# Spare products, copies, mixture pieces and weight sums moved in the first units of a fused RWKV-7 and mixture kernel

## The chip, the cores and the metric

The kernel runs on one core of a Trainium2 chip. The metric is the time of one execution on the device in microseconds, the median of several runs. The profile is of one execution and has its own time.

## The reference

Two blocks follow each other. The first is a recurrence over 768 time steps, for 4 batches of 8 heads, head size 40; each head keeps a 40 x 40 state S:

```
y[t]  = r[t] . S
Sa    = S . a[t]
S     = S * w[t] (by column) - outer(Sa, b[t]) + outer(v[t], k[t])
```

The outputs are laid side by side by head into x, 3072 rows (tokens) of 320. The second block is a mixture of 4 experts, all of them applied to every row, weighted by probabilities that are normalised by row:

```
p   = domain_probs / (sum(domain_probs) + 1e-9)
out = sum over e of p[:, e] * (relu(x @ w1[e]) @ w2[e])       w1[e]: 320 x 1024, w2[e]: 1024 x 320
```

Everything is float32.

## The kernel before

**Units.** The time axis is cut into 12 chunks of 64 steps. A unit is one chunk of two batches (all 16 heads of them), so there are 24 units; the units with an even and an odd number carry the two halves of the batches. Inside a chunk the recurrence is written as matrix products, with a triangular system of 64 x 64 per head to solve. A unit goes through these stages, each a generator that is advanced a step at a time:

- `within` (L412): what needs no state. The decays G are accumulated by a scan, turned to token order on TensorE (`pg`), inverted on VectorE (`gp`, a reciprocal), and multiplied into B and K, giving `n_tok` and `k_tok`. These are turned back (`turned`, tiles `pNT` and `pKT`, through `turn`, L359), and V and R as well (`turn_rv`, `pVT` and `pRT`, in units 0 to 2 on TensorE, later by VectorE's transposes). Products give the score matrices `pfe`, `pe` and `pc`, which are masked into F, ET and VC, and `pev`, copied to EV.
- `substitute` (L627), here called the solve: the 32 x 32 diagonal blocks of F are copied (`copy_blocks`, L619, for units 0 and 1), turned into M, and solved by forward substitution in Z. Units 0 and 1 are solved on VectorE, the later ones on GpSimd (POOL) while earlier units go on. The blocks below the diagonal go to the tile `below`.
- `merge` (L704): Z is turned into Qc and QTc; two products, `pY` and `pQ`, give the off-diagonal block of the inverse. QT collects it: the diagonal quarters from QTc (`diagonal`, on ScalarE for units 1 to 5, else on POOL), the others from `pQ`.
- `step` (L750): what needs the state. `prn` (not in the first chunk), `psat` and `pst`, `pxr`, then `pdy`, from which come the output Y and the next state. For the first four units Y is turned into xT by products with a matrix of ones (`pick`, built by `set_pick` with 14 selects on POOL, in the tile `sums` of the last expert); `pxT` is its result.
- the mixture: for units 0 and 1 by unit (`mixture_of_unit`, L930), then by chunk (`mixture_of_chunk`). Its work is cut into pieces in the list `todo`: an `ups(e)` makes the hidden layer of one expert (`ph`, then a relu on ScalarE to `hs`), a `down(e)` multiplies with w2 (`po`) and adds into `osb` with the gate on VectorE. From the second chunk on, the second product is a seven-product scheme, which needs sums of blocks of w2: `add_weights` (L984), 20 VectorE operations, of which some overwrite w2.

**Order.** For units 0 to 5 (`EARLY`) the order of TensorE is the order of the program; most operations on the other engines are pinned in the same way (`keep_in_program_order`), and the rest is placed by a scheduler. The first two units are written out by hand (L1150 to L1255), the others in a loop, in which `gap` (L1272) runs some of the sums (`sums_at`) and then one or two mixture pieces, to fill TensorE while the other engines work. In the solve of unit 1 the function `during_second` (L1217) puts pieces and parts of unit 2 between the 16 substitution steps. `keep_warm` (L1132) and `keep_warm_quadrants` issue products of the identity whose result nobody reads, called spare products here.

**Transfers.** Nearly all loads are issued in order by one queue (SP): the inputs of a unit some units ahead, the first weights in pieces (`load_piece`, 640 KB each), and w2 by expert (`load_w2`, 1280 KB each; that of the last expert only after the solve of unit 1, which uses its tile as room for M and Z).

All matrix products are issued from one helper line, L76, the turns from L79, so they are told apart by their tiles.

Of the kernel before, what the change touches and what calls it, by code (L numbers as in the profile page):

```python
# [15 lines left out]
def kernel(  # L16
# [38 lines left out]
    nc = tc.nc  # L55
# [303 lines left out]
    def turn(name, src, pinned=False):  # L359

        p = big(name)
        for j in range(NJ):
            ins = transpose(out=p[:, j * P:(j + 1) * P], in_=src(j), identity=ident[:])
            if pinned and j == 0:
                tc.keep_in_program_order(ins)
        return p
# [45 lines left out]
    def within(q):  # L412
# [69 lines left out]
        def turned(name, x):  # L482
            t = sb.tile([P, NJ, P], FP32, name=name, tag="turned", bufs=3)
            p = turn("p" + name, tok(x), q.u == 1)[:]
            for js in (slice(0, NJ // 2), slice(NJ // 2, NJ)) if q.u == 0 else (slice(0, NJ),):
                ins = nc.scalar.copy(out=t[:, js], in_=p.rearrange("p (j t) -> p j t", t=P)[:, js])
                if q.u < 2:
                    tc.keep_in_program_order(ins)
            return t
# [44 lines left out]
        if q.u > 0:  # L534
            ins = nc.scalar.copy(out=q.VC[:, :, 0:D], in_=token_V())
            if q.u == 1:
                tc.keep_in_program_order(ins)
# [30 lines left out]
        if q.u == 0:  # L568
            copy_F()
            yield  # L570
            KT = turned("KT", q.K)
        if q.apart or q.u == 0:
            p = banks("pe")
# [11 lines left out]
        if q.u < 2:  # L585
            selected(ET[:], of_slot, pe)
            copy_below(q)
# [4 lines left out]
        if q.u == 0:  # L592
            tc.keep_in_program_order(nc.scalar.copy(out=q.VC[:, :, 0:D], in_=token_V()))
        q.EV = EVs()
# [10 lines left out]
        if q.u == 0:  # L605
            VT = turn_rv()
            yield
# [11 lines left out]
    def copy_blocks(q):  # L619
        blocks = sb.tile([P, H, Q], FP32, name="blocks")  # L620
        for n, (i, s) in enumerate((i, s) for i in range(P // Q) for s in range(2)):
            move = nc.scalar.copy if n >= 5 else nc.vector.tensor_copy
            to, src = of_slot(blocks[quarter(i)], s), q.pf[s][quarter(i), :, quarter(i % 2)]
            tc.keep_in_program_order(move(out=to, in_=src))
        return blocks

    def substitute(q, eng, during=None):  # L627
# [14 lines left out]
        if q.u < 2:  # L642
            unit_columns(nc.gpsimd)
            yield
            blocks = copy_blocks(q)
            yield
        else:
            blocks = sb.tile([P, H, Q], FP32, name="blocks")
            for i in range(P // Q):
                move = nc.scalar.copy if i >= 2 else nc.vector.tensor_copy  # L650
                tc.keep_in_program_order(move(out=blocks[quarter(i)], in_=q.F[quarter(i), :, quarter(i % 2)]))  # L651
            q.below = belows()
            for i in (1, 3):
                move = nc.scalar.copy if q.u <= EARLY else nc.gpsimd.tensor_copy
                tc.keep_in_program_order(move(out=q.below[quarter(i)], in_=q.F[quarter(i), :, 0:Q]))  # L655
# [48 lines left out]
    def merge(q):  # L704
# [16 lines left out]
        on_scalar = 0 < q.u <= EARLY  # L721
# [4 lines left out]
        def two_heads(name, lhsT, rhs, to):  # L726
            p = big(name)
            for n in range(NJ):
                for r in range(2):
                    matmul(  # L730
                        out=p[half(r), n * 2 * Q:(n + 1) * 2 * Q], lhsT=lhsT[half(r), 2 * n:2 * n + 2, :],
                        rhs=rhs[half(r), 2 * n:2 * n + 2, :], start=True, stop=True,
                    )
            for r in range(2):
                for y in range(2):
                    src = p[quarter(2 * r + y), 0:H * Q].rearrange("p (n two t) -> p n two t", two=2, t=Q)[:, :, y, :]
                    ins = nc.scalar.copy(out=of_slot(to[quarter(2 * r)], y), in_=src)  # L737
                    if q.u == 0:
                        tc.keep_in_program_order(ins)
# [190 lines left out]
    def mixture_of_unit(q):  # L930
# [3 lines left out]
        def ups(e):  # L934
# [6 lines left out]
            def piece():  # L941
                lead()
                hs[e] = [up_main(at + 2 * e, q.xT, P, ph[0])]
                hs[e].append(up_main(at + 2 * e + 1, q.xT, P, up_last(at + 2 * e + 1, q.xT, P)))
# [6 lines left out]
            piece.lead = lead  # L951
            return piece
# [14 lines left out]
        todo.append(ups(0))  # L967
        for e in range(E):
            todo.append(lambda e=e: down(e))
            if e + 1 < E:  # L970
                todo.append(ups(e + 1))
# [186 lines left out]
    keep_warm(8)  # L1158
# [10 lines left out]
    run(ws[0], 1)  # L1169
    set_pick()  # L1170
    run(solve)
    keep_warm(16)
    run(ws[0], 3)
    keep_warm(5)
    run(ws[0])
    run(norm, 1)
    keep_warm(4)
    run(ws[1], 1)
    keep_warm(20)
# [9 lines left out]
    keep_warm_quadrants(1)  # L1189
# [3 lines left out]
    run(ws[1], 1)  # L1193
# [13 lines left out]
    run(ws[1], 1)  # L1207
    run(solve, 1)
    run(s, 1)
# [7 lines left out]
    def during_second(j):  # L1217
        if j == 0:
            run(s)
        if j == 4:  # L1220
# [3 lines left out]
            mix(1)  # L1224
        if j == 8:
# [24 lines left out]
    run(m)  # L1250
    run(s, 2)
    run(ws[2])
# [6 lines left out]
    sums_at = {4 * 2 + n: 1 for n in range(1, 11)}  # L1259
    sums_at.update({4 * 4 + 3: 2, 4 * 5 + 0: 3, 4 * 5 + 1: 2, 4 * 5 + 2: 3})  # L1260
# [122 lines left out]
```

## Time and profile before

| | |
|---|---|
| median of 3 runs | 1106.63 us (1103.67 to 1109.6) |
| profiled execution | 1105.66 us |
| its span, first to last instruction | 1103.8 us |
| TensorE busy (PE) | 1077.6 us, 98% |
| VectorE (DVE), ScalarE (ACT), GpSimd (POOL) busy | 753.9, 367.1, 496.7 us |
| mean granted TensorE clock | 0.992 |
| DMA, mean | 111 GB/s, 122.18 MB |

Times in the views count from the first instruction. PE is the matrix products, PEld the weight loads, SPq the issue of a transfer on the SP queue. A row such as `L681 DVE TENSOR_TENSOR w<-w` names the line, the engine, the operation, and the tiles written and read. A float32 product appears as two rows, so 20 spare products are 40 rows. A bracket behind a row gives the idle time of the engine before it and what ended it; "issue" there means that the profile shows nothing that was waited for. The granted clock is a share of full speed.

### The profile page before, as it was taken

What the parts mean: (1) busy time and instruction counts of PE and PEld (TensorE: products, weight loads), DVE (VectorE), ACT (ScalarE), POOL (GpSimd) and SP (SyncE); (2) the same over time, 40 slices, a digit from 0 to 9 for tenths busy, and PEclk for the clock granted to TensorE, in tenths of its full rate; (3) what the DMA queues carried; (4) which work ended last, traced back from release to release, by engine and by line L of the source; (5) the groups of instructions that cost most, each with busy time, mean ns of one, the idle gap of its engine ahead of it and who ended that gap; (6) DMA issues with size and microseconds to landing.
All of it is one profiled execution on the core that took longest, in us unless ns stands there. A gap on an engine that the chain in (4) does not pass through costs nothing.

```text
span 1103.8 us, 38664 instructions
## 1 busy us (share of the span) xinstructions
PE 1077.6 (98%) x16158; PEld 963.5 (87%) x16158; DVE 753.9 (68%) x1546; ACT 367.1 (33%) x998; POOL 496.7 (45%) x1257
## 2 busy tenths in 40 slices
PE   7899899999999999999999999999999999999998
PEld 6777778888999899999989989999998989988887
DVE  7665578887776767767768677767777677543343
ACT  3343555243233243233232342332332342321110
POOL 6215465672653643744634635536537447330000
PEclk8999999999999999999999999999999999999999
DMA  7876625434454364353454443453543532222320
GB/s 145 210 191 172 141 53 151 96 92 122 99 124 112 102 142 106 93 146 93 102 124 114 102 120 89 125 126 78 132 102 84 147 85 67 97 71 77 101 81 12
DMA packets 268868, 122.18 MB, mean 111 GB/s; under 512 B 213736, under 2 KB 242072, under 8 KB 268696
## 3 DMA queue, kind: packets, MB, share of 16 engines
q1 hardware_dynamic: 264872, 119.02, 43.1%
q8 instruction: 127, 2.08, 0.8%
q10 hardware_dynamic: 3824, 0.71, 0.4%
q14 instruction: 45, 0.37, 0.1%
HBM read 111.79 MB, written 3.93 MB: 105 GB/s over the span
## 4 chain that ended last, share of the span: by engine, by line
PE 86%; DVE 5%; ACT 3%; POOL 2%; SPq 2%; issue 2%; DMA 1%; DVEq 0%; ACTq 0%; POOLq 0%
PE ph L76 36%; PE p L76 28%; PE po L76 3%; PE pdy L76 3%; PE psat L76 2%; PE pxr L76 2%; PE prn L76 1%; PE pc L76 1%; PE pQ L76 1%; PE pfe L76 1%; PE warm L76 1%; POOL Z L697 1%; PE pev L76 1%; PE pe L76 1%; PE pY L76 1%
## 5 line engine op out<-in xcount | busy, mean ns | idle before, releaser
L76 PE MATMUL ph<-xT,w1p 128*128 128x256 f32 (+3 forms) x3040 | 443.5, 376 | 3.1 <-issue 1.5
L76 PEld LDWEIGHTS ph<-xT,w1p 64*64 64x64 f32 (+1 forms) x3040 | 336.8, 161 | 70.9 <-issue 25.5
L697 POOL TENSOR_TENSOR Z<-Z 128x31 f32<-128x31 f32 (+7 forms) x704 | 259.0, 368 | 55.2
L1028 DVE TENSOR_TENSOR a<-hs 128x512 f32<-128x512 f32 x220 | 151.9, 708 | 108.3 <-ACT hs L907 108.3
L681 POOL TENSOR_TENSOR Z<-M,Z 128x62 f32<-128x62 f32 (+7 forms) x352 | 142.6, 405 | 150.2 <-DVE M L672 124.3
L907 ACT ACTIVATE hs<-ph 128x512 f32<-128x512 f32 (+1 forms) x208 | 115.1, 564 | 223.4 <-PE ph L76 222.4
L76 PE MATMUL p<-sums,a 128*128 128x160 f32 x1056 | 164.9, 299 | 0.0
L76 PEld LDWEIGHTS p<-sums,a 128*128 128x128 f32 x1056 | 152.8, 190 | 2.2
L920 DVE SCALAR_TENSOR_TENSOR osb<-p,gate,osb 128x320 f32<-128x320 f32 (+1 forms) x243 | 108.3, 482 | 57.7 <-PE p L76 53.4
L76 PE MATMUL p<-w,a 128*128 128x160 f32 x704 | 106.0, 301 | 0.4 <-ACT hs L907 0.4
L76 PE MATMUL p<-w,hs 128*128 128x160 f32 x704 | 102.9, 299 | 0.0
L76 PEld LDWEIGHTS p<-w,hs 128*128 128x128 f32 x704 | 100.2, 190 | 2.2
L76 PEld LDWEIGHTS p<-w,a 128*128 128x128 f32 x704 | 98.3, 190 | 3.3 <-ACT hs L907 3.3
L655 POOL COPY below<-F 32x256 f32<-32x256 f32 x36 | 17.3, 480 | 178.9 <-ACT F L563 177.8
L657 DVE STREAM_TRANSPOSE M<-blocks 128x1024 f32<-128x1024 f32 x23 | 45.4, 1975 | 39.5 <-ACT blocks L651 38.9
L819 ACT COPY RS<-pxr 64x256 f32<-64x256 f32 x88 | 32.3, 367 | 103.6 <-DVE SX L410 42.0
L719 POOL COPY QT<-QTc 32x256 f32<-32x256 f32 x76 | 43.0, 566 | 36.1 <-DVE QTc L711 26.0
L600 ACT COPY EV<-pev 64x160 f32<-64x160 f32 x96 | 23.4, 287 | 87.5 <-PE pev L76 87.0
L478 DVE RECIPROCAL gp<-gp 128x320 f32<-128x320 f32 x23 | 49.5, 2152 | 0.7
L709 DVE STREAM_TRANSPOSE Qc<-Z 128x256 f32<-128x256 f32 x23 | 14.5, 629 | 43.7 <-POOL Z L697 43.6
L737 ACT COPY QT<-pQ 32x128 f32<-32x128 f32 x96 | 24.7, 257 | 58.3 <-PE pQ L76 56.5
L76 PE MATMUL pdy<-VC,k_tok 64*64 64x104 f32 (+1 forms) x768 | 38.2, 260 | 1.4 <-issue 1.4
(169 smaller groups left out, 1382.2 us busy)
## 6 DMA issues: line engine op xcount, KB each, us to landing
w1p<-in_moe_w_dram SPq DMA_DIRECT2D x95, 512.0 KB
w1p<-in_moe_w_dram SPq DMA_DIRECT2D x190, 64.0 KB
w<-in_moe_w_dram SPq DMA_DIRECT2D x4, 1280.0 KB
sums<-in_moe_w_dram SPq DMA_DIRECT2D x9, 512.0 KB
natW<-in_w_dram SPq DMA_DIRECT2D x48, 80.0 KB
natB<-in_b_dram SPq DMA_DIRECT2D x48, 80.0 KB
natK<-in_k_dram SPq DMA_DIRECT2D x48, 80.0 KB
out_dram<-osb SPq DMA_DIRECT2D x46, 80.0 KB
```

The lines of the kernel that those rows point to most:

```text
L76: return stated(nc.tensor.matmul(**k))
L478: pin(nc.vector.reciprocal(out=gp[:], in_=gp[:]))
L600: ins = nc.scalar.copy(out=of_slot(q.EV[half(p)], i ^ p)[:, :, 0:D], in_=pev[i][half(p)])
L657: ins = nc.vector.transpose(out=M[:], in_=cols)
L681: ins = eng.tensor_tensor(out=Z[:, 1:3, 0:n, j + 1:Q], in0=M[:, j:j + 2, None, j + 1:Q].to_broadcast([P, 2, n, m]), in1=Z[:, here, 0:n, j: ...
L697: eng.tensor_tensor(out=z[:, 0], in0=z[:, 0], in1=z[:, x], op=ALU.add)
L719: tc.keep_in_program_order(move(out=q.QT[quarter(i), :, quarter(i % 2)], in_=QTc[quarter(i)]))
L737: ins = nc.scalar.copy(out=of_slot(to[quarter(2 * r)], y), in_=src)
L819: nc.scalar.copy(out=RS[half(s), x ^ s::2], in_=prs[x][half(s)].rearrange("p (j i) t -> p j i t", i=2),)
L907: nc.scalar.activation(out=h[:, i * HF // 2:(i + 1) * HF // 2, 0:n], in_=ph[i][:], func=ACTF.Relu,)
L920: nc.vector.scalar_tensor_tensor(out=to, in0=p, scalar=sc, in1=to, op0=ALU.mult, op1=ALU.add)
L1028: nc.vector.tensor_tensor(out=t[:], in0=x, in1=y, op=op)
```

## The change

The change has seven parts, nearly all in the first two units.

1. Spare products: four and two go into the turn `pNT` of unit 0 (behind its second and fourth transpose), six behind the turn `pKT`; the counts elsewhere change from 14, 8, 16, 5, 4, 20 to 14, 9, 7, 3, 24, and one pair of `keep_warm_quadrants` goes.
2. In unit 0, V and R are turned ahead of `pev`, `copy_below` comes behind EV's copies, and `set_pick` behind the masks of unit 0.
3. `copy_blocks` gives the four copies of one bank to VectorE and the four of the other to ScalarE, where VectorE had five and ScalarE three.
4. `pQ` of unit 0 goes to two banks, and two of the four QT copies to VectorE.
5. Order in the merges: the step of unit 1 that holds `pNT` and `pKT` comes behind `pdy` of unit 0, `pfe` behind `pxT`, and the copies for ET ahead of the relus. In the merge of unit 1 one `ups` is cut in two (`first`, `second`) and run there, so that the `down` behind it moves one gap ahead.
6. For units 2 to 5, the copies to `below` and the diagonal copies to QT go from ScalarE to POOL.
7. The 20 sums lie in 15 gaps (1, 2 or 1 each) where they lay in 14 (1 each, then 2, 3, 2, 3).

The diff, without unchanged context:

```diff
-    def turn(name, src, pinned=False):
+    def turn(name, src, pinned=False, spare={}):
...
+            if spare.get(j):
+                keep_warm(spare[j])
...
-            p = turn("p" + name, tok(x), q.u == 1)[:]
+            p = turn("p" + name, tok(x), q.u == 1, {1: 4, 3: 2} if q.u == 0 and name == "NT" else {})[:]
...
-            if q.u == 1:
+            if q.u < PADDED:
                 tc.keep_in_program_order(ins)
...
             KT = turned("KT", q.K)
+            keep_warm(6)
...
             selected(ET[:], of_slot, pe)
-            copy_below(q)
+            if q.u == 1:
+                copy_below(q)
...
             tc.keep_in_program_order(nc.scalar.copy(out=q.VC[:, :, 0:D], in_=token_V()))
+            VT = turn_rv()
+            yield
         q.EV = EVs()
...
         if q.u == 0:
-            VT = turn_rv()
-            yield
+            copy_below(q)
...
-        for n, (i, s) in enumerate((i, s) for i in range(P // Q) for s in range(2)):
-            move = nc.scalar.copy if n >= 5 else nc.vector.tensor_copy
-            to, src = of_slot(blocks[quarter(i)], s), q.pf[s][quarter(i), :, quarter(i % 2)]
-            tc.keep_in_program_order(move(out=to, in_=src))
+        for i in range(P // Q):
+            for s, move in enumerate((nc.vector.tensor_copy, nc.scalar.copy)):
+                to, src = of_slot(blocks[quarter(i)], s), q.pf[s][quarter(i), :, quarter(i % 2)]
+                tc.keep_in_program_order(move(out=to, in_=src))
...
-                move = nc.scalar.copy if q.u <= EARLY else nc.gpsimd.tensor_copy
-                tc.keep_in_program_order(move(out=q.below[quarter(i)], in_=q.F[quarter(i), :, 0:Q]))
+                tc.keep_in_program_order(nc.gpsimd.tensor_copy(out=q.below[quarter(i)], in_=q.F[quarter(i), :, 0:Q]))
...
-        on_scalar = 0 < q.u <= EARLY
+        on_scalar = q.u == 1
...
-            p = big(name)
+            apart = q.u == 0 and name == "pQ"
+            ps_ = banks(name) if apart else [big(name)] * 2
...
-                    ins = nc.scalar.copy(out=of_slot(to[quarter(2 * r)], y), in_=src)
+                    move = nc.vector.tensor_copy if apart and r else nc.scalar.copy
+                    ins = move(out=of_slot(to[quarter(2 * r)], y), in_=src)
...
-            def piece():
+            def first():
                 lead()
                 hs[e] = [up_main(at + 2 * e, q.xT, P, ph[0])]
+
+            def second():
                 hs[e].append(up_main(at + 2 * e + 1, q.xT, P, up_last(at + 2 * e + 1, q.xT, P)))
...
-            return piece
+            return [first, second] if q.u == 0 and e == E - 1 else [piece]
...
-    keep_warm(8)
+    keep_warm(9)
     run(solve, 1)
...
+    run(solve)
+    run(ws[0], 2)
+    keep_warm(7)
+    run(ws[0], 1)
+    keep_warm(3)
+    run(ws[0])
     set_pick()
-    run(solve)
-    keep_warm(16)
-    run(ws[0], 3)
-    keep_warm(5)
-    run(ws[0])
     run(norm, 1)
-    keep_warm(4)
     run(ws[1], 1)
-    keep_warm(20)
+    keep_warm(24)
...
-    keep_warm_quadrants(1)
     run(ws[1], 1)
     run(m)
     keep_warm_quadrants(1)
-    run(ws[1], 1)
     load_w2(1)
...
     run(s, 1)
     run(ws[1], 1)
+    run(s, 1)
+    run(ws[1], 1)
     run(solve, 1)
-    run(s, 1)
+    run(ws[1], 1)
     mixture_of_unit(units[0])
...
             go(load_raw(begin(3), "W"))
-            mix(1)
-        if j == 8:
+        if j in (6, 8):
             mix(1)
...
     run(m)
+    mix(1)
     run(s, 2)
+    mix(1)
     run(ws[2])
...
-    sums_at = {4 * 2 + n: 1 for n in range(1, 11)}
-    sums_at.update({4 * 4 + 3: 2, 4 * 5 + 0: 3, 4 * 5 + 1: 2, 4 * 5 + 2: 3})
+    sums_at = {4 * 2 + n: 1 if n < 6 or n > 10 else 2 for n in range(1, 16)}
```

More of the change, by code (lines that the diff above doesn't have):

```diff
@@ L730, in two_heads @@
                     matmul(
-                        out=p[half(r), n * 2 * Q:(n + 1) * 2 * Q], lhsT=lhsT[half(r), 2 * n:2 * n + 2, :],
+                        out=ps_[r][half(r), n * 2 * Q:(n + 1) * 2 * Q], lhsT=lhsT[half(r), 2 * n:2 * n + 2, :],
                         rhs=rhs[half(r), 2 * n:2 * n + 2, :], start=True, stop=True,
@@ L735, in two_heads @@
                 for y in range(2):
-                    src = p[quarter(2 * r + y), 0:H * Q].rearrange("p (n two t) -> p n two t", two=2, t=Q)[:, :, y, :]
-                    ins = nc.scalar.copy(out=of_slot(to[quarter(2 * r)], y), in_=src)
+                    src = ps_[r][quarter(2 * r + y), 0:H * Q].rearrange("p (n two t) -> p n two t", two=2, t=Q)[:, :, y, :]
+                    move = nc.vector.tensor_copy if apart and r else nc.scalar.copy
+                    ins = move(out=of_slot(to[quarter(2 * r)], y), in_=src)
                     if q.u == 0:
@@ L949, in piece @@
                     load_w2(e + 2)
-            piece.lead = lead
-            return piece
+            def piece():
+                first()
+                second()
+            piece.lead = first.lead = lead
+            return [first, second] if q.u == 0 and e == E - 1 else [piece]
         def down(e):
@@ L965, in down @@
                 stores.append(lambda: store(q, q.osb))
-        todo.append(ups(0))
+        todo.extend(ups(0))
         for e in range(E):
@@ L970, in mixture_of_unit @@
             if e + 1 < E:
[L971 removed]
+                todo.extend(ups(e + 1))
     def of_w2(e, q, x):
```

## The prediction

> **What bounds the kernel now.** I read the page first (busy time, then the slices), then the busy time by stretches, then the first 115 us engine by engine in order of time. The page:
>
> ```profile
> PE 1077.6 (98%) x16158; PEld 963.5 (87%) x16158; DVE 753.9 (68%) x1546; ACT 367.1 (33%) x998; POOL 496.7 (45%) x1257
> PE   7899899999999999999999999999999999999998
> ```
>
> TensorE is the bound, but not everywhere. Busy time by stretches (second column the length, then PE, its weight loads, DVE, ACT, POOL, granted clock, DMA share, GB/s):
>
> ```profile
> 0.00:28.00 28.00, 20.60 (x234) 18.81 (x234) 22.04 (x56) 8.56 (x25) 17.90 (x56) 0.88 0.75 147
> 28.00:56.00 28.00, 25.12 (x423) 22.54 (x416) 18.57 (x47) 10.37 (x32) 5.70 (x9) 0.94 0.83 210
> 56.00:83.00 27.00, 24.44 (x327) 19.38 (x325) 17.77 (x40) 11.20 (x33) 5.31 (x7) 0.94 0.71 190
> 83.00:110.00 27.00, 25.32 (x359) 20.98 (x354) 15.95 (x38) 9.18 (x29) 16.28 (x48) 0.94 0.62 175
> 330.00:1104.00 774.00, 769.17 (x11114) 695.52 (x11112) 511.98 (x1043) 236.47 (x624) 330.40 (x843) 1.00 0.40 101
> ```
>
> From 330 us on TensorE idles 4.8 us of 774 at full clock; its work there is the same in both kernels. So the change is worth what it takes out of the first 140 us (idle TensorE, half-clock stretches, spare products on the path), and each microsecond won there should reach the end.
>
> TensorE in order of time (start, length, count; the bracket is idle time before and who ended it):
>
> ```profile
> 12.91 0.69 PE L76 MATMUL pfe<-NT,AT 64*64 64x64 f32 x32 [0.55 <-ACT NT L486]
> 15.85 1.13 PE L76 MATMUL pe<-AT,KT 64*64 64x64 f32 x32 [1.66 <-ACT KT L486]
> 16.92 6.36 PE L76 MATMUL warm<-ident 128*128 128x128 f32 x32
> ...
> 28.00 0.65 PE L79 MATMUL pp<-ident,sums 24*128 24x24 f32 x4
> ...
> 31.75 4.98 PE L76 MATMUL warm<-ident 128*128 128x128 f32 x40
> 36.66 0.68 PE L76 MATMUL pY<-QTc,below 64*64 64x64 f32 x16
> ...
> 51.02 2.65 PE L76 MATMUL ph<-xT,w1p 64*64 64x128 f32 x32 [1.42 <-ACT xT L861]
> ...
> 57.99 0.30 PE L76 MATMUL pev<-VC,ET 64*64 64x40 f32 x2 [1.74 <-DVE gl L450]
> 58.71 0.61 PE L76 MATMUL pev<-VC,ET 64*64 64x40 f32 x27 [0.41 <-POOL ET L500]
> ...
> 59.80 6.24 PE L76 MATMUL po<-w,hs 128*128 128x320 f32 x16
> ```
>
> And VectorE:
>
> ```profile
> 31.45 0.45 DVE L711 STREAM_TRANSPOSE QTc<-Qc 128x256 f32<-128x256 f32 x1
> ...
> 66.08 0.55 DVE L918 TENSOR_SCALAR osb<-po,gate 128x320 f32<-128x320 f32 x1 [6.14 <-PE po L76]
> ```
>
> Three things to see. First, QTc is ready at 31.90, yet pY, which needs it, starts at 36.66: it queues behind 20 spare products (40 rows, 4.98 us). Second, TensorE waits 1.74 + 0.41 us before pev of unit 1, because ACT makes ET's copies only after four hs activations; the next po runs at half clock (6.24 us; the same form at full clock takes 4.47). Third, VectorE's solve of unit 1 sits 6.14 us behind that po.
>
> **Part by part.**
>
> *Blocks split by bank.* Five DVE copies (0.258 us each from 13.65) then three on ACT to 15.40 become four and four on different banks: done at 13.65 + 4 x 0.258 = 14.7. The solve of unit 0 (15.44 to 31.90, 16.46 us) ends at about 31.25: -0.65. Unit 1 gets the same.
>
> *Spare products in the first N turn.* Four warm products (0.244 us each at full clock) fit between n_tok's halves (11.0 to 11.95 against 11.92 now), two before pfe end at 12.9 (pfe starts at 12.91), six before pe end at about 15.6 (pe starts at 15.85). On the path: 0 to +0.1. They are for the clock: here it is 0.5 from 15.3 to 22.2, 29.0 to 32.4, 59.7 to 63.2 and 94.0 to 97.4, each stretch one or two times 3.4 us and each after 3.4 us with only 1.2 to 2.2 us idle in pieces.
>
> [...]
>
> Stretches with 1.4 us idle (42.7 to 46.1, 49.5 to 52.9) stayed at full clock, so the rows give no sharp bound either, and I count half a window where I am unsure.
>
> *Moved set_pick, V and R turns, below.* POOL's 14 selects (4.26 us) leave the place ahead of ET and go behind VC's selects, about 23.8 to 28.8, before QTc: hidden; ET is ready near 19.0. pev and pc come out at about 19.7 and 21.0. Then pp needs the probabilities, issued by SP until 21.5; the nearest row for landing is 2.6 to 3.0 us (rawW 2.57, natB 3.04), so pp near 24.2, though all the trace proves is "by 28.0". V and R turns of unit 1 (0.9) and 24 warm products (5.86) follow: 31.6 at full clock, 33.3 with one half-clock window (+1.7), 36.2 if pp goes at 28.0. I take pY at 32.3 (31.4 to 36.2), from 36.66.
>
> *QT copies on two engines.* The DVE pair stands behind gp and the 2.15 us reciprocal of unit 1, which need pg, now right after pY: pg ends 33.5 to 34, gp 0.5, reciprocal 2.15, copies 0.55: psat at 37.2 (36.7 to 40.8) against 39.63. So of 4.4 us at pY 2.4 are left.
>
> *psat to the first ph*, 11.39 us now: pNT/pKT go behind pdy (0.87), pfe/pe behind pxT (0.9, of which half comes back ahead of ph), n_tok and k_tok leave the way of SX (0.66), xT comes ahead of the blocks copies on ACT (0.85). That makes 8.4 if a 1.44 us stall inside pdy (released by "issue") is gone too, 9.8 if not; I take 9.1. First ph at 46.3: -4.7.
>
> *ACT's order for unit 1* (ET's copies before hs): removes 2.15 idle and 1.77 of half clock: po of expert 0 ends 8.6 earlier, near 57.4. The gate add stands two steps later, so the 6.14 us DVE wait goes; next late is gp of unit 2, behind pg on TensorE. From there TensorE's row (23.4 us to pY of unit 1, 0.41 idle) sets the pace; DVE's solve without its waits ends about a microsecond ahead. -8.6 carried to pY of unit 1, near 80.9.
>
> *Pieces in the second merge.* ph x8 and ph x16 fill the 1.27 us before psat, where 1.7 us of half clock followed. The price: the last po (4.3 us) no longer covers what follows pdy, and it waits itself for w of expert 3, issued by SP at 94.67 behind 16 raw loads; the traffic that can be its own runs at 309 to 385 GB/s from 97 to 100 us, so I put its landing near 100.3, 10.8 after pY (89.46), and let it move with the SP queue, which runs without a break from natB on (74.90, released by n_tok). From pY to unit 1's first ph it was 22.8 us. Laid out again from pY: po 10.8 to 15.1, pdy to 16.9, Y and state on DVE to 18.6, gp, half of G and the reciprocal to 21.7, the rest of G, n_tok and k_tok to 23.1, pKT and pc to 24.2; TensorE has only pg and pxT (2.0) from 16.9 on, so it idles some 3.5 us before pNT. That is +1.4, with a half-clock window +3.1, and -0.5 if w is early: +2.2 taken.
>
> *below and QT copies of units 2 to 5 to POOL.* ACT loses 0.82 on F to pQ (idle 2.13 before pQ at 122.04): -0.8 once; later units have almost no idle. POOL gains 4 x 0.57 + 2 x 0.48 = 3.2 us a unit, inside its own wait for M (10.18 us, then 5.38 and 5.39). Without that cover: up to 3.2 a unit, four times.
>
> *Weight sums spread.* 20 sums of 0.82 to 0.87 us, same count, in 15 gaps instead of 14, finished one gap before use or just ahead of it. DVE is near 80% busy there and TensorE idles 0.1 to 1.6 us in each 27 us: 0 (-0.5 to +1).
>
> Sum: -4.7 - 3.9 + 2.2 - 0.8 = -7.2 on the profiled execution's 1105.66 (span 1103.8 and 1.86 around it): 1098.5. The median 1106.63 lies 0.97 above that execution, so 1099.4; I say 1099.
>
> **Rivals.** *The head's gain stays in the head* (0.2): probabilities late (pp at 28.0), the "issue" stall back, a half-clock window more. psat 40.8, ph 9.8 later at 50.6 (-0.4), then -3.9 + 3.1 - 0.8: -2.0, 1104.6. For it: three steps that only bounds price. Against: the 2.15 us and the 6.14 us waits go anyway.
>
> *The last po blocks pdy* (0.09), slower than before. Place: second merge, po of expert 3 now ahead of pdy, which the next state, xT and n_tok of unit 3 hang on. If SP's issues do not come earlier, w lands at 100.3 as before, po ends at 104.6, unit 1's first ph starts at 113.6 + 1.7 = 115.3 against 112.24: +3.1 - 0.8 = +2.3, 1109. It decides from a landing at about 98; each microsecond later costs one. Against: all that SP waits for comes earlier.
>
> *The spare products do not hold the clock*: the windows at 15 and 29 stay; about +1.7, 1101, still inside the main case (0.64). The remaining 0.07 are new waits in units 2 to 9, whose DVE and ACT lists are reordered; slower.
>
> **How the numbers follow.** A run of this kernel tells about 0.5% (5.5 us) from no change: faster means under 1101.1. Main case 0.64, its own range 1094 to 1102, and a little of the first rival: faster 0.66. Same: most of the first rival and half the second, 0.23. Slower: the rest, 0.11. Range 1093 to 1106: from all bounds favourable (psat 36.7, ph 45.1 for -5.9, then -3.9 - 0.5 - 0.8 and -0.5 from the sums, some -11.6 or 1095, less 2 for the spread of the median's runs, 1103.67 to 1109.6) to beyond the first rival.
>
> **What would show it.** Right: pY near 32, a wait of psat on DVE's QT copy behind the reciprocal, first ph near 46, no wait before pev, po of expert 0 near 4.5 us, pY of unit 1 near 81, an idle of 2 to 4 us before pNT of unit 3, the 330 us to end stretch unchanged. Wrong: pp still near 28, first ph after 50, po of expert 3 released by its DMA late, or TensorE idle of over 1 us a unit after 140 us.

## The result: slower, not faster, and the profile after

The changed kernel takes 1112.69 us (median, 1108.13 to 1115.88) where the kernel before took 1104.43 us beside it (1102.06 to 1109.6). The ratio on record, over all runs of both, is 1.0068, 95% interval 1.0047 to 1.0089; it is not the quotient of the two medians, which is 1.0075. In a second comparison it gave 1.0068 again (1.0044 to 1.0092). The prediction was 1099.0 with a range of 1093 to 1106. The profiled execution took 1112.64 us, span 1110.9, 7.1 us longer than the span before.

The page: TensorE has the same products and is busy 3 us more; the group that grew most is the first product of the mixture (443.5 us before), whose idle time ended by "issue" was 1.5 us before.

```profile
PE 1080.8 (97%) x16158; PEld 965.1 (87%) x16158; DVE 755.3 (68%) x1546; ACT 357.1 (32%) x974; POOL 511.0 (46%) x1281
...
L76 PE MATMUL ph<-xT,w1p 128*128 128x256 f32 (+3 forms) x3040 | 447.0, 378 | 5.7 <-issue 5.6
```

The busy time by the same stretches as before (start and end, length, PE, weight loads, DVE, ACT, POOL, granted clock, DMA share, GB/s):

```profile
0.00:28.00 28.00, 22.92 (x284) 21.40 (x285) 22.55 (x55) 11.89 (x35) 18.17 (x54) 1.00 0.78 151
28.00:56.00 28.00, 23.28 (x433) 20.57 (x431) 18.84 (x49) 8.97 (x29) 6.67 (x14) 0.76 0.84 210
56.00:83.00 27.00, 26.60 (x302) 21.51 (x293) 22.58 (x53) 9.57 (x27) 7.68 (x15) 1.00 0.87 233
83.00:110.00 27.00, 20.64 (x330) 16.22 (x330) 12.69 (x28) 8.72 (x29) 14.15 (x41) 0.94 0.58 147
330.00:1104.00 774.00, 773.21 (x11231) 699.19 (x11230) 517.08 (x1050) 237.43 (x629) 336.77 (x856) 1.00 0.40 101
```

The clock is now full in the first 28 us (0.88 before) and lower in the next (0.76 against 0.94). In 83 to 110 us TensorE is busy 20.64 us where it was 25.32: the second merge got worse. From 330 us on nothing is lost. TensorE in order of time:

```profile
22.80 0.63 PE L79 MATMUL pp<-ident,sums 24*128 24x24 f32 x4 [1.89 <-DMA sums<-in_moe_domain_probs_dram]
...
31.72 0.84 PE L76 MATMUL pY<-QTc,below 64*64 64x64 f32 x16 [1.91 <-DVE gl L452]
...
37.59 1.24 PE L76 MATMUL psat<-QT,EV 64*64 64x64 f32 x27 [1.11 <-DVE QT L743]
...
48.90 2.60 PE L76 MATMUL ph<-xT,w1p 64*64 64x128 f32 x32
...
84.33 0.62 PE L76 MATMUL pY<-QTc,below 64*64 64x64 f32 x14 [0.53 <-DVE QTc L715]
...
96.00 6.26 PE L76 MATMUL po<-w,hs 128*128 128x320 f32 x16 [2.34 <-DMA w<-in_moe_w_dram]
...
109.28 0.63 PE L79 MATMUL pNT<-ident,n_tok 128*128 128x128 f32 x4 [2.88 <-DVE n_tok L471]
...
110.93 4.04 PE L76 MATMUL ph<-xT,sums 64*64 64x128 f32 x32
```

The second merge in the kernel before:

```profile
89.41 0.62 PE L76 MATMUL pY<-QTc,below 64*64 64x64 f32 x13
...
104.33 4.47 PE L76 MATMUL po<-w,hs 128*128 128x320 f32 x16
...
109.97 0.60 PE L79 MATMUL pNT<-ident,n_tok 128*128 128x128 f32 x4
...
112.24 2.60 PE L76 MATMUL ph<-xT,sums 64*64 64x128 f32 x32
```

pY of unit 1 starts at 84.33 (89.41 before): the head did give 5.1 us. Then the last `po` waits 2.34 us for w of expert 3 and runs at half clock (6.26 us; 4.47 at full clock), TensorE idles 2.88 us before pNT, and ph of unit 1 runs at half clock too (4.04 against 2.60). From pY to that ph it is 26.6 us, 22.8 before. By pfe of unit 2 (117.48, before 117.35) the head's gain is gone.

The rest is lost between 183 and 330 us, at two places. Between pQ of units 4 and 5 it is 3.2 us: a stall before ph at 216.63 takes 2.14 us (1.53 before), with 3.4 us of half clock from 216.4 on (e12 below is about it). Between pQ of units 5 and 9 it is 5.0 us. VectorE and then TensorE, 256 to 312 us:

```profile
256.05 0.81 DVE L1006 TENSOR_TENSOR w<-w 128x640 f32<-128x640 f32 x1
262.30 0.71 DVE L249 STREAM_TRANSPOSE AT<-rawA 128x512 f32<-128x512 f32 x1 [5.44 <-DMA rawA<-in_a_dram]
262.93 1.25 DVE L1040 TENSOR_TENSOR a<-hs 128x512 f32<-128x512 f32 x2
264.10 0.68 DVE L528 TENSOR_TENSOR AT<-AT,G 128x512 f32<-128x512 f32 x1
264.70 0.55 DVE L926 SCALAR_TENSOR_TENSOR osb<-p,gate,osb 128x320 f32<-128x320 f32 x1
265.17 0.68 DVE L1040 TENSOR_TENSOR a<-hs 128x512 f32<-128x512 f32 x1
265.77 0.38 DVE L926 SCALAR_TENSOR_TENSOR osb<-p,minus_gate,osb 128x160 f32<-128x160 f32 x1
```

```profile
266.25 0.87 PE L76 MATMUL ph<-xT,w1p 64*64 64x256 f32 x11 [1.95 <-issue]
...
312.37 0.87 PE L76 MATMUL ph<-xT,w1p 64*64 64x256 f32 x11 [1.48 <-issue]
```

The bracket says "issue", but the order of time tells more: `osb<-p,minus_gate` ends at 266.15 and ph starts at 266.25. At the second stall osb ends at 312.27 and ph starts at 312.37. The second ph tile shares three PSUM buffers (tag "mm") with the products p that osb reads, so these times fit a ph that waits until VectorE has read one of them. VectorE is late since a transpose AT<-rawA stands ahead of `a` and `osb` in its list and waits 5.44 us for a load that SP issues behind twelve xT transfers and a w1 piece. In the kernel before the operations at the first place stand the other way round, and the transpose waits for nothing; at the second it stands behind the first two `a` but ahead of the osb adds there too, and waits 0.40 us:

```profile
258.02 1.29 DVE L1028 TENSOR_TENSOR a<-hs 128x512 f32<-128x512 f32 x2 [1.13 <-ACT hs L907]
259.57 0.55 DVE L920 SCALAR_TENSOR_TENSOR osb<-p,gate,osb 128x320 f32<-128x320 f32 x1 [0.25 <-PE p L76]
...
262.81 0.38 DVE L920 SCALAR_TENSOR_TENSOR osb<-p,minus_gate,osb 128x160 f32<-128x160 f32 x1
263.10 0.70 DVE L249 STREAM_TRANSPOSE AT<-rawA 128x512 f32<-128x512 f32 x1
...
302.61 0.71 DVE L249 STREAM_TRANSPOSE AT<-rawA 128x512 f32<-128x512 f32 x1 [0.40 <-DMA rawA<-in_a_dram]
```

### The profile page after: what moved, and what is told of

It is laid out like the page before. It is cut to its first block, busy times and chain, and to the rows that moved or that the text cites. A ratio compares the mean times of both kernels' runs of the same rounds, so it can differ in the third digit from the quotient of the medians.

```text
span 1110.9 us, 38662 instructions
## 1 busy us (share of the span) xinstructions
PE 1080.8 (97%) x16158; PEld 965.1 (87%) x16158; DVE 755.3 (68%) x1546; ACT 357.1 (32%) x974; POOL 511.0 (46%) x1281
## 4 chain that ended last, share of the span: by engine, by line
PE 81%; DVE 7%; POOL 5%; ACT 3%; issue 2%; DMA 1%; SPq 0%; DVEq 0%; POOLq 0%; ACTq 0%
PE ph L76 34%; PE p L76 27%; POOL Z L701 3%; PE pdy L76 3%; PE po L76 2%; PE psat L76 2%; POOL Z L685 2%; PE pxr L76 2%; PE pfe L76 1%; PE prn L76 1%; PE pQ L76 1%; PE pc L76 1%; DVE M L661 1%; PE pNT L79 1%; PE pev L76 1%
## 5 line engine op out<-in xcount | busy, mean ns | idle before, releaser
L659 POOL COPY below<-F 32x256 f32<-32x256 f32 x44 | 21.7, 492 | 188.2 <-ACT F L565 186.7
L723 POOL COPY QT<-QTc 32x256 f32<-32x256 f32 x92 | 51.1, 555 | 58.1 <-DVE QTc L715 49.2
L779 ACT COPY SN<-prn 128x256 f32<-128x256 f32 x44 | 14.7, 373 | 80.0 <-DVE RH L774 80.0
```

Of the source, the lines that this page charges most:

```text
L723: tc.keep_in_program_order(move(out=q.QT[quarter(i), :, quarter(i % 2)], in_=QTc[quarter(i)]))
```

## The experiments

One table serves all of them. A column "pQ of unit n" is the start of that product in the profiled execution, less its start in the kernel before: it tells where time is won or lost. The ratio is the one on record, of all the kernel's runs to those of the kernel before on the same chip: it tells how much. The two must not be mixed: single executions of one kernel differ by up to 10 us (the run "copies for unit 2 only" was profiled in its fastest execution, 1098.77 of 1098.77 to 1107.18).

| kernel | last po | unit 1 | unit 2 | unit 5 | unit 9 | unit 23 | ratio, 95% |
|---|---|---|---|---|---|---|---|
| changed | ahead of pdy | -5.1 | -0.7 | +2.1 | +7.1 | +7.2 | 1.0068 (1.0047-1.0089) |
| changed, again (e13) | ahead | -5.2 | +2.0 | +3.7 | +6.0 | +8.1 | 1.0068 (1.0044-1.0092) |
| e1 second half back | behind | -3.7 | -7.4 | -5.6 | -5.2 | -4.4 | 0.9978 (0.9961-0.9995) |
| e2 rawA early | ahead | -5.6 | +0.3 | +3.6 | +8.0 | +9.9 | 1.0081 (1.0056-1.0107) |
| e3 sums, copies back | ahead | -3.2 | +4.0 | +4.5 | +7.5 | +10.7 | 1.0071 (1.0054-1.0089) |
| e4 before + merge pieces | ahead | -0.9 | +6.8 | +6.9 | +11.4 | +12.7 | 1.0081 (1.0061-1.0101) |
| e5 last po behind pdy | behind | -3.1 | -6.2 | -2.0 | -1.8 | -1.4 | 0.9971 (0.9956-0.9987) |
| e6 w3 ahead of raw | ahead | -2.7 | -2.0 | -0.2 | +0.7 | +1.0 | 1.0009 (0.9996-1.0022) |
| e7 copies unit 2 only | behind | -6.3 | -8.6 | -8.2 | -8.1 | -8.1 | 0.9977 (0.9964-0.9991) |
| e8 head alone | behind | -2.8 | -2.8 | -2.5 | -2.2 | -2.3 | 0.9972 (0.9959-0.9984) |
| e9 rawA late | ahead | -8.1 | +0.6 | +2.3 | +2.0 | +4.2 | 1.0048 (1.0029-1.0067) |
| e14 the same again | ahead | -4.0 | -1.3 | +0.4 | +2.1 | +4.2 | 1.0059 (1.0035-1.0083) |
| e10 spare before waits | behind | -7.6 | -7.7 | -5.8 | -4.3 | -4.3 | 0.9983 (0.9965-1.0001) |
| e11 w3 ahead, best | behind | -7.5 | -7.0 | -4.7 | -3.3 | -2.8 | 0.9943 (0.9922-0.9964) |
| e12 sums spread kept | behind | -5.3 | -7.3 | -4.0 | -3.4 | -2.1 | 0.9985 (0.9971-1.0000) |
| e15 po behind, w3 ahead | behind | -4.9 | -7.5 | -1.4 | -1.0 | +0.6 | 0.9966 (0.9951-0.9981) |

From unit 1 to unit 2, the stretch of the second merge, the seven traces with the po ahead and the loads in the old order lose 2.7 to 8.7 us, e6 loses 0.7, and the eight with the po behind lose at most 0.5.

The first theory was that the list of VectorE makes most of the loss and the second merge the rest; rival A, that the second merge alone does; rival B, that the weight sums or POOL's copies do. Which list a kernel has is read from the built program, before it runs.

**e1: second half of the up-projection back behind the merge.**

```diff
     run(s, 2)
-    mix(1)
     run(ws[2])
```

> The changed kernel, but the second half of expert 3's up-projection of unit 0 goes back behind the second merge (the mix after the step's second stage is taken out; all else stays). Built, VectorE's list of units 3 to 9 then has the order of the kernel before again: the a and osb operations stand ahead of the transpose AT<-rawA, and the last po stands behind pdy. Main theory (the loss is made at 210 to 315 us, where the transpose waits for rawA ahead of the osb adds that free a PSUM bank, and the second merge ate the head's gain): the stalls of 1.95 and 1.48 us before ph at 266 and 311 us go with their half-clock windows (about 4.5 us together), the wait of po for w of expert 3 (2.34 us) goes with its half clock (1.8 us): 1101 us, 1098 to 1104. Rival A (the loss is only the second merge's own waits and windows): 1106 to 1108. Rival B (the loss is in the spread weight sums or in POOL's added copies, which stay here): 1111 to 1113.

Measured 0.9978, 10 us under the changed kernel and inside the main theory's 1098 to 1104 (0.994 to 1.000 of before). No wait of po for w; the stalls at 266 and 312 us are gone. It does not separate merge and list, since both went back.

**e2: rawA issued early.**

```diff
-            go(load_raw(begin(u + 3), "W"))
+            go(load_raw(begin(u + 3), "WA"))
...
-            go(load_raw(units[u + 3] if ahead else begin(u + 3), "A" if ahead else "WA"))
+            if not ahead:
+                go(load_raw(begin(u + 3), "WA"))
```

> The changed kernel, with one thing more: for units 8 to 10 rawA is issued together with rawW, ahead of the twelve xT transfers on SP's queue, instead of behind them. Nothing of the second merge, the weight sums or POOL's copies is touched. Main theory: the 5.4 us waits of VectorE for rawA at 257 and 303 us go, and with them the stalls of TensorE before ph at 266 and 311 us (1.95 and 1.48 us) and their half-clock windows (1.2 us and less): 4 to 5 us faster than the changed kernel, 1107.5 to 1109; the stall at 216.6 us stays. Rivals A and B (the second merge; the weight sums and POOL's copies): 1112 to 1113, no change.

A miss: no gain (1.0081). The waits for rawA are gone, but the scheduler then put AT<-rawA and its product even earlier, ahead of RT, and pc waited for that:

```profile
255.58 0.69 PE L76 MATMUL pc<-RT,VT 40*64 40x64 f32 x32 [2.22 <-DVE RT L249]
```

So the early load was no way to take the wait out alone: it changed the list again.

**e3: sums and copies of before.** Parts 6 and 7 undone in the changed kernel (the two `move` and `on_scalar` lines and `sums_at` of the diff above).

> The changed kernel with the weight sums in the gaps of before and the copies of below and QT of units 2 to 5 on ScalarE again (POOL's added copies out). Built, the transpose AT<-rawA of units 7 and 8 still stands ahead of the a and osb operations. Main theory: the stalls at 266 and 311 us stay; 1112, 1110 to 1114, the stall at 216.6 us perhaps 0.6 us shorter. Rival B (the sums or the copies cost the time): 1105 to 1107.

Measured 1.0071: parts 6 and 7 do not make the loss; rival B falls.

**e4: the merge pieces alone on the kernel before.** `first` and `second`, and the two `mix(1)` in the second merge.

> The kernel before with one part of the change alone: expert 3's up-projection of unit 0 in two pieces and both of them inside the second merge. Built, VectorE's list of units 2 to 9 is then that of the changed kernel, with AT<-rawA ahead of the a and osb operations. Main theory: the stalls at 266 and 311 us appear (about 4.5 us) and the second merge gets its waits with no gain of the head to pay for them (2 to 5 us): 1109 to 1114. Rival A (the merge's own waits alone): 1106 to 1109. Rival B (sums or copies): 1104 to 1105.

Measured 1.0081, 9 us: the pieces alone cost, within the noise, what the whole change costs (1.0068). pQ of unit 2 is 6.8 us late, with the po of expert 3 waiting 3.88 us for w; from unit 5 to the end 5.8 us more.

**e5: only the last po back.** In the built lists, what turns VectorE's list is neither piece but the `down` behind them, which moves one gap ahead, in front of pdy. So:

```diff
-        gap(0)
+        gap(0, 0 if u == 1 else None)
```

> The changed kernel with one move: the down-projection of expert 3 of unit 0 (the last po, 8 products) goes from in front of pdy of unit 1 to behind pdy and pg, where it was before. Both halves of the up-projection stay in the second merge, the rest of the change stays too. Built, VectorE's list of units 2 to 9 is that of the kernel before again. Main theory now (the last po's place sets both the wait for w and the order in which the later lists come out): from pQ of unit 1 to pQ of unit 2 some 27 to 28 us (35.8 in the changed kernel, 31.3 before), from pQ of unit 4 to pQ of unit 8 at most 3 us more than before (8.2 in the changed kernel), the whole 0.994 to 0.998 of before. Rival A (the later loss has nothing to do with the lists and comes from what the second merge does to the clock and to the loads): the merge is won, 8 us are still lost in units 5 to 9, 1.002 to 1.006 of before. Rival C (the second half inside the merge is itself the fault): as the changed kernel, 1.005 or more.

Measured 0.9971: this one move is worth 10.7 us (1.0068 to 0.9971 of 1105 us). Rival C is out, and the merge is won as well as forecast: from pQ of unit 1 to pQ of unit 2 it takes 28.25 us, in the changed kernel 35.75 and (e13) 38.54. TensorE there:

```profile
98.30 0.66 PE L79 MATMUL pg<-ident,G 128*128 128x128 f32 x4
98.80 4.47 PE L76 MATMUL po<-w,hs 128*128 128x320 f32 x16
103.10 1.50 PE L76 MATMUL pxT<-Y,sums 128*128 128x128 f32 x12
104.44 0.60 PE L79 MATMUL pNT<-ident,n_tok 128*128 128x128 f32 x4
...
106.34 0.69 PE L76 MATMUL pc<-RT,VT 40*64 40x64 f32 x32 [0.86 <-DVE RT L249]
```

Behind pdy and pg, the 4.47 us of po cover the state, gp and its reciprocal on VectorE, and w has landed. From pY (86.31) to the first ph of unit 1 (106.85) it is 20.5 us, where the changed kernel needs 26.6.

**e6: w of expert 3 ahead of the raw loads, po still ahead of pdy.**

```diff
-    go(load_raw(units[3], "VR"))
     run(ws[2], 1)
...
     load_w2(3)
+    go(load_raw(units[3], "VR"))
     mix(1)
```

> The changed kernel with one move on SP's queue: the load of w of expert 3 goes ahead of the 16 loads of rawV and rawR of unit 3. The last po stays ahead of pdy. Built, VectorE's list of units 5 to 9 is then close to that of before (the a and osb operations mostly ahead of AT<-rawA). Main theory: the wait of po for w (2.34 us) and its half clock (1.8 us) go, and units 5 to 9 lose at most 3 us instead of 8: 0.995 to 1.000 of before. Rival A (the place of the last po costs by itself, whatever the lists): only the 4 us of the wait come back: 1.002 to 1.004. If rawV or rawR of unit 3 now come too late, a new wait before pc of unit 3 shows it.

Measured 1.0009, above the main theory's interval by little and below rival A's: 6.5 us of the changed kernel's loss come back. SP issues w at 86.19 instead of 89.20 and po no longer waits, but pNT does:

```profile
96.28 4.57 PE L76 MATMUL po<-w,hs 128*128 128x320 f32 x16
...
107.99 0.85 PE L79 MATMUL pNT<-ident,n_tok 128*128 128x128 f32 x4 [3.00 <-DVE n_tok L471]
```

The list of this kernel has most `a` and `osb` ahead of AT<-rawA, and units 5 to 23 lose 1.2 us, with the po ahead. So the po's place costs by itself (3 us of wait), and in this trace the later loss goes with the list, not with the place. The ratio takes back both together: how much of the 6.5 us is the wait for w and how much the list, it doesn't tell.

**e7: copies on POOL for unit 2 alone, old sums**, on top of e5 (`2 < q.u <= EARLY` in both places of part 6, `sums_at` of before).

> As the kernel with the last po behind pdy, with two parts of the change undone besides: POOL takes the copies of below and QT for unit 2 alone (units 3 to 5 have them on ScalarE again), and the weight sums lie in the gaps of before. Main theory: POOL's Z of unit 5 is no longer late, so Qc waits 0.6 us less and the stall before ph near 210 us (2.56 us with the second half put back, 1.53 before) shrinks by 1 to 2 us: 1 to 2 us faster than with the last po behind pdy alone. Rival B (copies and sums cost nothing): no difference.

In the trace the stall near 210 us shrinks to 1.52 us (2.52 in e5), in the ratio nothing does (0.9977 against 0.9971).

**e8: the head alone.** The changed kernel without the merge pieces, parts 6 and 7.

> The change without its later parts: no piece of unit 0's mixture is moved into the second merge, POOL's added copies and the weight sums are as before; what stays is the first 90 us (split copies, spare products, moved selects and turns, ScalarE's order for unit 1). VectorE's list of units 2 to 9 is that of before. Main theory: the head's gain of 5.1 us (pY of unit 1 at 84.3 instead of 89.4) reaches the end whole where the second merge doesn't change: 0.995 to 0.997 of before. Rival A (the second merge waits for w of expert 3 or for raw loads, whose queue doesn't come earlier by as much, and takes the gain back): 0.998 to 1.000.

Measured 0.9972, 3 us: the head's gain, 2.8 us at unit 1 in this execution, reaches the end nearly whole. Rival A falls for this kernel.

**e9 and e14: rawA later.** The cleanest test of the list: TensorE's list is unchanged, VectorE's differs in the place of two transposes.

```diff
-            go(load_raw(units[u + 3] if ahead else begin(u + 3), "A" if ahead else "WA"))
+            if not ahead:
+                go(load_raw(begin(u + 3), "W"))
+            if u not in (5, 6):
+                go(load_raw(units[u + 3], "A"))
             load(units[u + 3], "WBKV")
+            if u in (5, 6):
+                go(load_raw(units[u + 3], "A"))
```

> The changed kernel with one thing moved: in iterations 5 and 6 of the loop over the units, rawA is loaded later, behind natW, natB, natK and natV on SP's queue, instead of ahead of them. TensorE's list is the same; built, VectorE's list differs from the changed kernel's in nothing but the place of two transposes AT<-rawA with their products, which now come behind the a and osb operations (the lines that waited at 262 and 308 us). The data comes about 5 us later than in the changed kernel. Main theory (the place of AT<-rawA in VectorE's list ahead of the osb adds makes the later loss): the stalls before ph at 266 and 312 us (1.95 and 1.48 us) and the half clock behind them go, from pQ of unit 5 to pQ of unit 9 at most 1 us more than before (5.0 in the changed kernel); 4 to 5 us faster than the changed kernel, 1.002 to 1.004 of before. Rival A (the later loss comes from something that the second merge leaves behind, not from that list): no change or, with the data later, slower: 1.006 to 1.010.

```profile
259.24 1.29 DVE L1040 TENSOR_TENSOR a<-hs 128x512 f32<-128x512 f32 x2 [2.24 <-ACT hs L913]
...
264.03 0.38 DVE L926 SCALAR_TENSOR_TENSOR osb<-p,minus_gate,osb 128x160 f32<-128x160 f32 x1
...
268.56 0.71 DVE L249 STREAM_TRANSPOSE AT<-rawA 128x512 f32<-128x512 f32 x1 [2.48 <-DMA rawA<-in_a_dram]
```

The data comes later and the kernel is not slower: both stalls are gone, from unit 5 to 9 it loses -0.3 us. But by the ratios it is only 2.2 us better than the changed kernel in another comparison, half of the forecast. Therefore once more, beside the changed kernel itself (e13, which has no edit):

> The changed kernel itself, as the partner of the next run on the same chip. Main theory and rivals alike: 1.005 to 1.009 of before.

> The changed kernel with rawA of iterations 5 and 6 loaded behind natW to natV, as before, now beside the changed kernel on one chip. If the place of AT<-rawA ahead of the osb adds makes the later loss in most executions: 3 to 5 us faster than the run beside it. If the profiled execution overstates it: 1 to 2.5 us.

1.0059 against 1.0068: 1 us (0.5 us between the medians), with intervals that overlap, and 4.0 us between the two profiled spans (1111.9 and 1107.9). In the changed kernel's second profile the stalls were 1.23 and 1.07 us, and from unit 5 to 9 it lost 2.3 us, not 5.0; so the first profile had shown the list at its worst. By the traces units 5 to 23 lose 4.4 to 6.3 us with AT<-rawA first (five traces), 1.9 and 3.8 with it moved, 0.1 to 2.0 in the other nine. That the list makes the stalls is shown; that it is worth more than 1 to 2 us by the ratios is not.

**e10: spare products in the waits for the probabilities and for QT**, on top of e7.

```diff
     set_pick()
+    keep_warm(6)
     run(norm, 1)
...
     run(m)
-    keep_warm_quadrants(1)
+    keep_warm_quadrants(5)
```

> The kernel of the run with copies for unit 2 alone, with six spare products more ahead of pp and eight 64x256 products more behind pQ of unit 0, in TensorE's waits for the probabilities (1.8 to 2.5 us) and for QT (1.1 to 1.8 us). If the half clock of 24 to 30 us and of 33 to 44 us follows those waits and costs time at psat and pdy: 1 to 2 us faster than that run, 0.995 to 0.997 of before, with the clock at 1.0 from 14 to 40 us. Rival (the half clock there lies under waits for QTc and QT anyway): no change, 0.997 to 0.999, or 0.5 us slower because the added products run over the wait.

0.9983, no gain: the rival. The clock was 1.00 from 14 to 34 us but 0.50 from 34.0 to 37.4, and the products added behind pQ ran in that.

**e11: w of expert 3 ahead of the raw loads**, on top of e10, **and e15**, the same load on top of e5.

> The kernel of the run with spare products before the waits, with the load of w of expert 3 ahead of the 16 loads of rawV and rawR of unit 3 on SP's queue as well; the last po stays behind pdy. Main theory (with the head done early, the landing of w of expert 3 is what po waits for, 2.76 us in that run): the wait goes, 1 to 3 us faster than that run, 0.995 to 0.998 of before. Rival (the raw loads of unit 3 now come late, and pc of unit 3 or VT waits instead): 0.998 to 1.000.

> The changed kernel with the last po of unit 0 behind pdy and, on SP's queue, w of expert 3 ahead of rawV and rawR of unit 3. Built, VectorE's list of units 5 to 9 is that of before. If the load is what brought the last variant from 0.998 to 0.994: 0.994 to 0.996 of before (0.997 without that load). If it was something else: 0.996 to 0.999.

e11 is the fastest kernel of the study, 0.9943 (1101.48 against 1107.99 us), better than both the kernel before and the changed one. Where its 4 us over e10 come from stays open: in its profile the wait for w (2.76 us in e10) is gone, but 2.11 us before pev and 1.16 us before pc stand in its place, and e15 (0.9966) gains nothing that can be told from e5, which is what the second of its two forecasts gave. The load alone does not bring it.

**e12: sums spread, copies for unit 2 alone**, e7 with the change's `sums_at`.

> As the run with copies for unit 2 alone, but with the weight sums spread as in the change. It tells which of the two parts makes the stall before ph near 210 us longer (1.1 to 1.5 us in all kernels with neither part, 2.1 to 2.8 us in all with both). If the sums do it (one of them stands ahead of osb in VectorE's list): 2.1 us or more, and 0 to 1 us slower than the run with both undone. If POOL's copies do it (Z of unit 5 late, Qc waits for it): 1.1 to 1.6 us, and as that run.

```profile
212.00 4.74 PE L76 MATMUL ph<-xT,w1p 64*64 64x256 f32 x30 [2.03 <-issue]
```

2.03 us against 1.52 in e7, just under the 2.1 that the sums were given: the sums lengthen this stall. In the nine traces that have the spread sums and POOL's copies for units 2 to 5 it costs more, 1.7 to 4.9 us between pQ of units 4 and 5; in e12, with the spread sums and the copies for unit 2 alone, it is 1.3 us, in the six other traces, without the spread sums, 0.0 to 0.7. So that the copies add nothing is not shown. In the ratios (0.9985 against 0.9977) none of it can be told.

## Why the prediction was wrong

Its steps, in the first profile of the changed kernel, with pQ of unit n as the mark: predicted -8.6 to pY of unit 1, +2.2 in the second merge, -0.8 for ScalarE, 0 after that. Measured: -5.1 at unit 1, +4.4 from there to unit 2 (with the -0.8), +2.8 to unit 5, +5.0 to unit 9, +0.1 to the end: +7.2.

*Right.* pp at 22.80 (24.2 forecast), psat at 37.59 (37.2), and its wait is that for DVE's QT copy. pY at 31.72 (32.3) is right in part by luck: the forecast had it behind the spare products, but with pp 1.4 us early these ended at 29.81, and pY waited 1.91 us for VectorE, whose QTc ended at 31.58 (31.90 before; 0.3 us won, not 0.65). The clock of the first 28 us is full, at no cost. The idle before pQ of unit 2 fell from 2.13 to 1.33 us, the -0.8 of part 6, and POOL's added copies lie inside its wait for M. The 2.15 and 6.14 us waits of unit 1 went.

*Head, size off.* psat to the first ph took 11.3 us, not 9.1, though the 1.44 us stall inside pdy, which the forecast left half open, did not come in this execution: the clock was 0.50 from 32.1 to 45.7 us, from just behind a wait of 1.91 us before pY, with waits of 0.70, 1.11 and 0.45 us inside it. The forecast counted no half clock behind pY, since it saw no wait there. The first ph came at 48.90, not 46.3. The 3.9 us of unit 1 became 3.0, as ph waits 0.56 us for hs and pY 0.53 us for QTc. In all traces with this head pY of unit 1 (89.41 before; the forecast reads 89.46) lies 2.7 to 8.1 us ahead; the ratio of e8 says 3.

*The failed step is "Pieces in the second merge".* It had the mechanism (po uncovers VectorE's chain, and waits itself for w), and its layout is near the trace: po 10.8 us behind pY (11.67 measured), then 3.5 us idle before pNT (2.88). It priced the whole at +2.2. In this execution the first ph of unit 1 comes 26.60 us behind pY, +3.8, and half clock makes that ph 1.4 us longer: +5.2 to pfe of unit 2. Two terms were too small. Half clock was counted as half of one window; here it came twice, 1.8 us in po and 1.4 us in ph. And w was put 5.6 us behind its issue (94.67 to 100.3). In the seven traces with the po ahead and the old order of loads the po, which starts when w has landed, starts 6.3 to 7.7 us behind the issue, so 11.6 to 15.8 us behind pY. The issue itself came earlier with the head, as forecast, in the changed kernel (89.20, 5.5 us earlier); in e9, with the earliest pY (81.32), it came 8.9 us behind pY, where 4.9 to 6.5 was the rule of the other six, and TensorE waited 6.44 us: what the head won there was waited away. Over these seven traces the second merge lost 2.7 to 8.7 us against the kernel before where the sum had +1.4 (+2.2 - 0.8), so the first profile (+4.4) shows it at the mild end.

The rival called "the last po blocks pdy" had the place right and got 0.09 and 1109. Its condition did not hold: it needed SP's issues to come no earlier and w to land at 98 or later, and here w was issued 5.5 us earlier and po started at 96.00. The run with the load moved (e6) and the one with the po moved (e5) show the po's place worth 6.5 us and 10.7 us of what the changed kernel lost.

*What no step had.* The forecast was laid out from the first 115 us and the stretch from 330 us on; between pQ of units 2 and 9 this profile lost 7.8 us. Lists of units 2 to 9 were known to be reordered, and got 0.07 with no price. The po's place also turned VectorE's list, so this loss belongs in part to the same move: from unit 5 on e5 loses 0.5 us, the changed kernel 5.1 and 4.4, but e9 and e14 show only 1 to 2 us of it in the ratios. The forecast for "weight sums spread" was 0 (-0.5 to +1); by the trace of e12 it is 1.3 us, by the ratios 0 to 1. The transposes AT<-rawA ahead of the osb adds were in the list that could be read before any run, and rawA's late issue was in the trace of before; put together they point at stalls at these two places.

The ratios give -3 us for the head (e8) and +10.7 us for the po's place (e5 against the changed kernel), which makes up the measured loss (0.68%, 7.5 us). How the 10.7 us divide is known from traces alone, 7.5 to 10.3 us in the second merge and about 4 us of stalls later, and these differ from execution to execution.

## What to carry to other kernels

Where a piece of work is moved ahead of the instruction that a long chain starts from, ask first what it covered where it stood, and when its own data lands by the queue that issues it, not by the work that precedes it: here one down-projection (`po`, 4.47 us at full clock) in front of pdy instead of behind it cost 10.7 us. When a scheduler places part of the instructions, compare the built lists far behind the edit, and look for an operation that waits for a load in front of one that frees a buffer. Profile a kernel twice before a stall of 2 us is called a cost: many runs decide how much, traces only where.

## What was not expected of the hardware

*The clock.* In the changed kernel the clock went to half at 32.1 us, just behind a wait of 1.91 us, and stayed there for 13.7 us (to 45.7), with waits of 0.70, 1.11 and 0.45 us inside. In e8 half clock from 43.6 to 50.4 us began inside one wait of 2.51 us (41.83 to 44.34):

```profile
42.00:44.00 2.00, 0.00 (x0) 0.00 (x0) 0.00 (x0) 0.00 (x0) 0.00 (x0) 0.89 0.72 88
44.00:46.00 2.00, 1.66 (x33) 1.42 (x32) 0.00 (x0) 0.00 (x0) 0.00 (x0) 0.50 0.68 119
46.00:48.00 2.00, 2.00 (x13) 1.99 (x11) 1.68 (x6) 0.59 (x1) 0.00 (x0) 0.50 0.77 143
48.00:50.00 2.00, 2.00 (x11) 2.00 (x11) 0.00 (x0) 0.59 (x1) 0.00 (x0) 0.50 0.36 60
```

The traces say more when they are cut into stretches of 3.41 us that end where the clock changes (its pieces are whole multiples of that length: the first five in the kernel before last 10.24, 6.83, 6.83, 3.41 and 27.31 us), here from 6 to 125 us in all 17 traces. Of 397 stretches at full clock with under 0.8 us of idle TensorE none was followed by half clock, of 36 with 1.4 to 2.0 us idle 25 were, and of 23 with 2.0 us or more all were. Of 53 at half clock with under 0.4 us idle 51 were followed by full clock, of 20 with more none. So what went with half clock is the idle time within such a stretch, not the length of one wait, and between 1.1 and 2.0 us it was uncertain: in the kernel before a stretch with 1.13 us idle (25.65 to 29.06) was followed by half clock and one with 1.44 us (42.72 to 46.13) was not; of the wait of 2.30 us before po in e14, 1.9 us lay in one stretch, and the clock stayed full; the 2.34 us in the changed kernel lay in one stretch, and half clock followed.

*A stall inside pdy of unit 0.* In 12 of the 17 traces one product of pdy waits 0.4 to 2.8 us, released by "issue", though its neighbours with the same operands ran before:

```profile
44.34 0.33 PE L76 MATMUL pdy<-SX,n_tok 64*64 64x104 f32 x1 [2.51 <-issue]
```

It stands behind 469 or 471 rows of TensorE's products in all twelve, before and after the change, though a different product stands there. It is absent in the first profile of the changed kernel, in e2, e9, e10 and e11. Over the executions it adds from nothing to 2.8 us to the head. The queue table of the changed kernel has a kind called "instruction":

```profile
q8 instruction: 128, 2.10, 0.8%
```

That is 16 KB a packet (2.10 MB in 128). In every one of the 17 traces the third of these packets ends between 39.1 and 44.4 us, and the product behind 469 (471) rows starts 1.2 to 2.0 us after that end; without its wait it would have started between 1.5 us ahead of that end and 1.9 us behind it. This fits a wait for that packet closely. That the product's own instruction comes late with it is the author's reading: no run moved the packet alone, so it is argued, not shown.
